# Four attention layers on one core: finishing each item's output later, spreading the Q/K projection, projecting V once, and zeroing on another engine

## The chip, the cores and the metric

One core of a Trainium2 chip. The metric is the device time of one execution in microseconds (us), on the slowest core, which here is the only one. Each profile also gives the clock that was granted to TensorE (PE), as a share of full speed, averaged over the run or over a stretch. In this case that clock takes only the values 0.5 ("cold") and 1.0 ("warm") at any moment (the traces of the two kernels have 244 stretches at each and none at another value), so a mean of 0.93 says that 14% of the time was cold. A stretch of time at 0.5 is called a cold spell below.

## The reference, cut to what matters

```python
def _A_ref(x, wqkv, wo):             # windowed layer; B is the same without the mask ("dense")
    qkv = (x @ wqkv).reshape(B, S, 3, H, Dh) ...      # S = 2048, D = 640, H = 32, Dh = 20
    scores = einsum("bhqd,bhkd->bhqk", q, k) * Dh**-0.5
    mask = (idx[:,None] - idx[None,:] >= 0) & (idx[:,None] - idx[None,:] < 256)
    p = softmax(where(mask, scores, -1e9))
    return einsum("bhqk,bhkd->bhqd", p, v) ... @ wo
x = x + A(layernorm(x)); x = x + B(layernorm(x))      # and both once more: four layers
```

## The kernel before

Everything stays in SBUF. A layer normalises x and transposes it to `xnT`. It then goes through eight groups `g` of four heads. In a group, each *item* is one block of 512 queries for two heads. It runs over its key blocks of 128 keys: 16 in a dense layer, 4 or 6 in a windowed one. For each key block it does S on PE (two heads of 32 rows each), exp on ScalarE (ACT), masks on VectorE (DVE), and PV on PE. V carries a column of ones, so PV also gives the softmax's sum. After the last key block comes the item's *tail*: copy out of PSUM, four transposes, and a division per head.

```python
        for g in range(G):                                       # 8 groups
            for tb in range(NT):                                 # V of this group: 80 columns wide
                vps = psA.tile([P, 4 * DH], F32, ...)
                for dc in range(KD): nc.tensor.matmul(vps[:], lhsT=xnT[...], rhs=stage[..., 80 cols])
                nc.vector.tensor_copy(out=v_g[:, tb, :, 0:DH], in_=vps[...])
            for which in range(2):                               # Q and K of this group
                for qsb in range(NQSB):
                    pps = psA.tile([P, QSB], F32, ...)
                    for dc in range(KD): nc.tensor.matmul(pps[:], lhsT=wpad[:, dc, g, :], ...)
                    nc.vector.tensor_copy(out=qkT[:, which, ...], in_=pps[:])
            for qsb in range(NQSB):
                for s in range(2):                               # one item
                    oT_ps = psB.tile([32, 2, QSB], F32, ...)
                    for ki, kc in enumerate(kcs):
                        # S: two matmuls, 32 rows each
                        for j in range(2):
                            nc.tensor.matmul(s_ps[:, j, c0:c1],
                                lhsT=qkT[slot : slot + 32, 1, ...], rhs=qkT[slot : slot + 32, 0, ...],
                                tile_position=(slot, 0), ...)
                        pt = ptp.tile([P, 2, QSB], BF16, ...)    # 3 buffers
                        if windowed and (c0 > 0 or c1 < QSB):
                            nc.gpsimd.memset(pt[:], 0.0)         # the whole tile
                        nc.scalar.activation(out=pt[:, :, c0:c1], in_=s_ps[:, :, c0:c1], func=ACT.Exp)
                        # ... masks on VectorE ...
                        for j in range(2):
                            nc.tensor.matmul(oT_ps[0 : DH + 1, j, :], lhsT=v_g[:, kc, 2*s+j, :], rhs=pt[:, j, :], ...)
                    # tail: two copies, then four transposes from psB, each with two divisions
                    for j in range(2): nc.vector.tensor_copy(out=oT_sb[...], in_=oT_ps[0 : DH + 1, j, :])
                    for qb in range(4):
                        tr_ps = psB.tile([P, 64], BF16, ...)
                        nc.tensor.transpose(out=tr_ps[:], in_=oT_sb[0:64, ...], identity=ident[0:64, 0:64])
                        # ... reciprocal and scaling for two heads ...
        # ... output projection, residual add
```

The softmax here doesn't subtract the row's maximum and nothing guards it: scores larger than these inputs give would overflow.

## Time and profile before

4597.9 us is the median of 15 runs (4588.2 to 4606.5). The runs agree well, and every one has a mean clock near 0.82. This is where the profiled run spends it; attention runs from a layer's first exp to its last, and a boundary is what lies between:

| stage | us | clock |
|---|---|---|
| start to first exp | 61.7 | |
| windowed attention, first / second | 711.0 / 707.2 | 0.72 / 0.72 |
| dense attention, first / second | 1391.1 / 1405.6 | 0.88 / 0.86 |
| three boundaries between layers | 88.7, 86.7, 87.4 | |
| end | 60.5 | |

From the page of the kernel before: the clock in 40 slices (in tenths), the shares of the chain that ended last, by engine, and four of the costliest groups (busy us, mean ns of one, then idle time ahead of them and what ended most of it).

```profile
PEclk8776777888988888988867677777888898888888
PE 44%; ACT 26%; DVE 15%; issue 12%; POOL 2%; DMA 1%; ACTq 0%; POOLq 0%; DVEq 0%
L235 ACT ACTIVATE pt<-s_ps 128x1024 bf16<-128x1024 f32 (+2 forms) x2752 | 2429.5, 915 | 1785.4 <-PE s_ps L224 715.6
L267 PE MATMUL oT_ps<-pt,v_g 128*21 128x512 bf16 x5504 | 1920.6, 461 | 351.9 <-ACT pt L235 182.3
L276 DVE CAST oT_sb<-oT_ps 21x512 bf16<-21x512 f32 x512 | 347.8, 679 | 2000.4 <-PE oT_ps L267 1996.9
L234 POOL MEMSET pt<- 128x1024 bf16 x704 | 645.8, 952 | 1080.6 <-PE oT_ps L267 1019.0
```

The exp, the largest single job, leaves ScalarE idle for 1785 us. The chain of the end goes through VectorE and "issue" for 27% of the time, which is what handing work to and fro costs. And the clock row contains sixes and sevens in the two windowed stretches: there PE was busy 73% of the time at a mean clock of 0.72, in the dense ones 85 and 86% at 0.88 and 0.86.

### The profile page before, as it was taken

Reading aid. Unit: us, or ns where it says so; the run is one execution under the profiler, and the core shown is the slowest. Engines: PE = TensorE matmul, PEld = TensorE weight load, DVE = VectorE, ACT = ScalarE, POOL = GpSimd, SP = SyncE. Lnnn points to the kernel's source line nnn. Section 1 sums busy time; section 2 is a strip of 40 time slices with the busy share of each in tenths; the row PEclk is TensorE's granted clock in tenths of the full one; section 3 lists DMA queues with packets and bytes.
Section 4 is the critical chain, followed back from the end, with each engine's and each line's share of the span. In section 5 each row is a group of like instructions: output and inputs, shape, how many; then the busy total and the mean of one; then the engine's idle time right before and its main releaser. Section 6 shows DMA issues by size and latency. Waiting matters only on the chain.

```text
span 4599.8 us, 48782 instructions
## 1 busy us (share of the span) xinstructions
PE 3690.3 (80%) x17152; PEld 1242.5 (27%) x17152; DVE 1673.3 (36%) x7465; ACT 2458.6 (53%) x2824; POOL 666.8 (14%) x748
## 2 busy tenths in 40 slices
PE   5777777788888888888777777768888888888886
PEld 2222222322222222222322222232222222222223
DVE  6555556421222212212465555563212212212223
ACT  2222322467677676676422232225676676676773
POOL 3434443000000000000034444420000000000000
PEclk8776777888988888988867677777888898888888
DMA  1000000000000000000000000000000000000000
GB/s 52 1 1 1 1 1 22 8 1 0 1 1 1 1 0 1 1 1 22 1 8 1 1 1 1 22 8 1 1 1 1 1 1 1 1 1 1 1 0 23
DMA packets 9622, 21.46 MB, mean 5 GB/s; under 512 B 160, under 2 KB 6816, under 8 KB 9376
## 3 DMA queue, kind: packets, MB, share of 16 engines
q1 hardware_dynamic: 9376, 18.35, 1.1%
q8 instruction: 134, 2.20, 0.2%
q14 instruction: 112, 0.92, 0.1%
HBM read 15.73 MB, written 2.62 MB: 4 GB/s over the span
## 4 chain that ended last, share of the span: by engine, by line
PE 44%; ACT 26%; DVE 15%; issue 12%; POOL 2%; DMA 1%; ACTq 0%; POOLq 0%; DVEq 0%
ACT pt L235 26%; PE oT_ps L267 24%; PE s_ps L224 9%; PE pps L193 6%; DVE oT_sb L276 5%; POOL pt L234 2%; PE vps L176 2%; DVE o_sb L293 2%; PE y_ps L310 2%; DVE rz L290 1%; DVE pt L259 1%; PE tr_ps L282 1%; DVE pt L246 1%; DVE v_g L183 1%; DVE x_sb L317 1%
## 5 line engine op out<-in xcount | busy, mean ns | idle before, releaser
L235 ACT ACTIVATE pt<-s_ps 128x1024 bf16<-128x1024 f32 (+2 forms) x2752 | 2429.5, 915 | 1785.4 <-PE s_ps L224 715.6
L267 PE MATMUL oT_ps<-pt,v_g 128*21 128x512 bf16 x5504 | 1920.6, 461 | 351.9 <-ACT pt L235 182.3
L224 PE MATMUL s_ps<-qkT 32*128 32x512 bf16 (+3 forms) x5504 | 1146.6, 386 | 213.1 <-ACT pt L235 183.6
L276 DVE CAST oT_sb<-oT_ps 21x512 bf16<-21x512 f32 x512 | 347.8, 679 | 2000.4 <-PE oT_ps L267 1996.9
L267 PEld LDWEIGHTS <-v_g 128*21 128x21 bf16 x5504 | 502.4, 101 | 1159.7 <-issue 913.1
L234 POOL MEMSET pt<- 128x1024 bf16 x704 | 645.8, 952 | 1080.6 <-PE oT_ps L267 1019.0
L224 PEld LDWEIGHTS <-qkT 32*128 32x128 bf16 x5504 | 283.7, 92 | 1298.0 <-issue 1273.1
L293 DVE TENSOR_SCALAR o_sb<-tr_ps,rz 128x20 bf16<-128x20 bf16 x2048 | 403.4, 222 | 24.4
L172 POOL MEMSET v_g<- 128x64 bf16 x32 | 12.2, 381 | 2437.7 <-PE oT_ps L267 2437.7
L282 PE MATMUL tr_ps<-ident,oT_sb 64*128 64x64 bf16 x1024 | 175.0, 212 | 209.1 <-DVE oT_sb L276 111.9
L290 DVE RECIPROCAL rz<-tr_ps 128x1 f32<-128x1 bf16 x2048 | 302.7, 159 | 100.1 <-PE tr_ps L282 75.3
L246 DVE TENSOR_TENSOR pt<-pt,mask_ge 128x256 bf16<-128x256 bf16 x512 | 146.8, 287 | 361.6 <-ACT pt L235 361.1
L200 DVE CAST qkT<-pps 128x512 bf16<-128x512 f32 x256 | 177.0, 691 | 121.9 <-PE pps L193 121.7
L282 PEld LDWEIGHTS <-oT_sb 64*128 64x128 bf16 x1024 | 79.4, 97 | 496.2 <-DVE oT_sb L276 184.5
L183 DVE CAST v_g<-vps 128x80 bf16<-128x80 f32 x512 | 118.2, 236 | 251.1 <-PE vps L176 233.2
L176 PE MATMUL vps<-stage,xnT 128*128 128x80 bf16 x2560 | 187.4, 218 | 22.0 <-DVE v_g L183 11.5
L176 PEld LDWEIGHTS <-xnT 128*128 128x128 bf16 x2560 | 139.5, 108 | 82.7 <-issue 56.8
L193 PE MATMUL pps<-xnT,wq_pad 128*128 128x512 bf16 x640 | 149.8, 391 | 0.0
L193 PE MATMUL pps<-xnT,wk_pad 128*128 128x512 bf16 x640 | 143.4, 379 | 0.0
L141 ACT ACTIVATE rstd<-mv,eps_t 128x1 f32<-128x1 f32 x64 | 18.8, 294 | 221.0 <-DVE mv L139 117.9
L259 DVE TENSOR_TENSOR pt<-pt,mask_lt 128x256 bf16<-128x256 bf16 x448 | 118.7, 283 | 3.0
L310 PE MATMUL y_ps<-wo_sb,oTd 128*128 128x320 bf16 x640 | 119.0, 316 | 0.0
(33 smaller groups left out, 700.0 us busy)
## 6 DMA issues: line engine op xcount, KB each, us to landing
stage<-in_A_wqkv_dram SPq DMA_DIRECT2D x2, 2400.0 KB, 12.0
stage<-in_B_wqkv_dram SPq DMA_DIRECT2D x2, 2400.0 KB, 9.0
x_sb<-in_A_x_dram SPq DMA_DIRECT2D x1, 2560.0 KB, 9.8
out_dram<-x_sb SPq DMA_DIRECT2D x1, 2560.0 KB, 8.7
wo_sb<-in_A_wo_dram SPq DMA_DIRECT2D x2, 800.0 KB, 9.8
wo_sb<-in_B_wo_dram SPq DMA_DIRECT2D x2, 800.0 KB, 4.5
```

The source lines that it names most:

```text
L176: nc.tensor.matmul(vps[:], lhsT=xnT[:, dc, tb * P : (tb + 1) * P], rhs=stage[:, dc, 2 * D + g * 4 * DH : 2 * D + (g + 1) * 4 * DH], start= ...
L193: nc.tensor.matmul(pps[:], lhsT=wpad[:, dc, g, :], rhs=xnT[:, dc, qsb * QSB : (qsb + 1) * QSB], start=(dc == 0), stop=(dc == KD - 1),)
L224: nc.tensor.matmul(s_ps[:, j, c0:c1], lhsT=qkT[slot : slot + 32, 1, kc * P : (kc + 1) * P], rhs=qkT[slot : slot + 32, 0, qsb * QSB + c0 : ...
L234: nc.gpsimd.memset(pt[:], 0.0)
L235: nc.scalar.activation(out=pt[:, :, c0:c1], in_=s_ps[:, :, c0:c1], func=ACT.Exp)
L246: nc.vector.tensor_tensor(out=pt[:, :, qb_diag * P : (qb_diag + 1) * P], in0=pt[:, :, qb_diag * P : (qb_diag + 1) * P], in1=mview, op=ALU. ...
L267: nc.tensor.matmul(oT_ps[0 : DH + 1, j, :], lhsT=v_g[:, kc, h_in_g, :], rhs=pt[:, j, :], start=(ki == 0), stop=(ki == len(kcs) - 1),)
L276: nc.vector.tensor_copy(out=oT_sb[32 * j : 32 * j + DH + 1, :], in_=oT_ps[0 : DH + 1, j, :],)
L282: nc.tensor.transpose(out=tr_ps[:], in_=oT_sb[0:64, qb * P : (qb + 1) * P], identity=ident[0:64, 0:64],)
L290: nc.vector.reciprocal(out=rz[:], in_=tr_ps[:, 32 * j + DH : 32 * j + DH + 1])
L293: nc.vector.tensor_scalar_mul(out=o_sb[:, qsb * 4 + qb, hh * DH : (hh + 1) * DH], in0=tr_ps[:, 32 * j : 32 * j + DH], scalar1=rz[:, 0:1],)
L310: nc.tensor.matmul(y_ps[:, i, 0 : D // 2], lhsT=oTd[:, dc, :], rhs=wo_sb[:, dc, i * (D // 2) : (i + 1) * (D // 2)], start=(dc == 0), stop= ...
```

## The change

Its intent: keep PE and ScalarE going across the ends of items and groups. The tail of an item is emitted after the next item's loop, with its own PSUM pool. A group's Q and K are projected in four portions during the group before. V is projected for all heads at once at the layer's start, into a store with zero columns, so that both heads add into one 64-row PSUM tile and one copy empties it. The zeroing of `pt` moves from GpSimd (POOL) to VectorE and covers only the columns that the exp leaves out. Cut to its core:

```diff
-    vp = ctx.enter_context(tc.tile_pool(name="vp", bufs=2))
+    psC = ctx.enter_context(tc.tile_pool(name="psC", bufs=2, space=bass.MemoryType.PSUM))
+    v_all = big.tile([P, NT, H // 2, 96], BF16, name="v_all", tag="v_all")
+    def emit_tail(item):
+        oT_ps, hA, qsb, s = item
+        nc.vector.tensor_copy(out=oT_sb[:], in_=oT_ps[:])        # one copy for both heads
+        for qb in range(4): ...                                  # transposes (from psC), divisions as before
...
+        if lidx == 0:
+            nc.gpsimd.memset(v_all[:], 0.0)
+            # ... and the columns of ones
+        for tb in range(NT):
+            for h2 in range(2):
+                vps = psC.tile([P, 16 * DH], F32, name="vps", tag="c")      # 320 columns
...
+        emit_qk_proj(0, list(range(NQSB)))
+        pending = None
         for g in range(G):
-            # V projection of the group, QK projection of the group
             for qsb in range(NQSB):
                 for s in range(2):
-                    oT_ps = psB.tile([32, 2, QSB], F32, name="oT_ps", tag="o")
+                    oT_ps = psB.tile([64, QSB], F32, name="oT_ps", tag="o")
...
-                        if windowed and (c0 > 0 or c1 < QSB):
-                            nc.gpsimd.memset(pt[:], 0.0)
+                        if windowed and c0 > 0:
+                            nc.vector.memset(pt[:, :, 0:c0], 0.0)
+                        if windowed and c1 < QSB:
+                            nc.vector.memset(pt[:, :, c1:QSB], 0.0)
...
-                                oT_ps[0 : DH + 1, j, :],
-                                lhsT=v_g[:, kc, h_in_g, :],
+                                oT_ps[:],
+                                lhsT=v_all[:, kc, hA // 2, 32 * j : 32 * j + 64],
...
-                    # tail at once
+                    if pending is not None:
+                        emit_tail(pending)
+                    pending = (oT_ps, hA, qsb, s)
+                if g + 1 < G:
+                    emit_qk_proj(g + 1, [qsb])
```

## The prediction

> **What bounds the kernel now.** I read the page's 40 slices, then busy time by stage, then ScalarE's order of time inside one dense and one windowed layer, then the chain of waits over the same stretches. The stages (attention of the windowed layer, boundary, attention of the dense layer, last projection), from the windows view:
>
> ```profile
> 60.00:775.00 715.00, 523.92 (x2501) 182.74 (x2500) 399.36 (x1795) 214.65 (x354) 322.78 (x357) 0.72 0.01 4
> 775.00:859.00 84.00, 62.79 (x442) 38.44 (x443) 70.25 (x312) 4.71 (x16) 0.00 (x0) 0.80 0.03 11
> 859.00:2265.00 1406.00, 1197.07 (x5235) 368.54 (x5233) 304.11 (x1351) 1004.98 (x1027) 5.81 (x11) 0.88 0.01 2
> 4548.00:4600.00 52.00, 27.01 (x223) 19.09 (x222) 26.35 (x91) 0.00 (x0) 0.00 (x0) 0.93 0.15 51
> ```
>
> After the stretch: length, busy us of PE, weight load, DVE, ACT, POOL, then the granted clock. The two layer pairs repeat, so the span is about 60 + 2 x 715 + 3 x 84 + 2 x 1407 + 45 = 4600. No engine fills either attention stage (ACT 1005 of 1406 is the most, if matmul busy is not trusted), so both are held by a chain.
>
> Dense layer, one item (one query block of two heads, 16 key blocks), ScalarE's timeline:
>
> ```profile
> 1141.76 1.94 ACT L235 ACTIVATE pt<-s_ps 128x1024 bf16<-128x1024 f32 x2 [3.00 <-PE oT_ps L267]
> 1144.86 14.47 ACT L235 ACTIVATE pt<-s_ps 128x1024 bf16<-128x1024 f32 x14 [1.17 <-PE s_ps L224]
> 1161.44 1.94 ACT L235 ACTIVATE pt<-s_ps 128x1024 bf16<-128x1024 f32 x2 [2.11 <-PE oT_ps L267]
> ```
>
> 16.41 us of exponentials, about 4 us of idle per item. What PE does in that idle, from the chain:
>
> ```profile
> 1138.80 0.58 PE s_ps L224
> 1139.38 0.16 PE tr_ps L282
> 1139.55 0.54 PE s_ps L224
> 1140.09 0.18 PE tr_ps L282
> 1140.29 0.17 DVE rz L290
> 1140.45 0.14 DVE o_sb L293
> 1140.59 0.04 issue
> 1140.63 3.58 PE oT_ps L267 x8
> ```
>
> The four transposes of the finished item stand in PE's queue ahead of the next item's PV matmuls, and wait for VectorE's evacuation and for each other's buffers. Then 8 PV matmuls run at 3.58/8 = 0.45 us each, against 0.26 in the steady loop: the clock has dropped. Items in this stretch repeat every 20.58 us (they start at 1099.46, 1120.05, 1140.63). Between groups ScalarE is idle another 18.29 us, during the V and QK projections.
>
> Windowed layer, start of one item, ScalarE waiting for GpSimd's zeroing:
>
> ```profile
> 311.94 0.12 PEld L267 LDWEIGHTS <-v_g 128*21 128x21 bf16 x2 [0.78 <-PE tr_ps L282]
> 311.97 2.72 PE L267 MATMUL oT_ps<-pt,v_g 128*21 128x512 bf16 x6 [0.68 <-DVE o_sb L293]
> 313.04 2.74 POOL L234 MEMSET pt<- 128x1024 bf16 x3 [4.46 <-PE oT_ps L267]
> 314.02 1.49 ACT L235 ACTIVATE pt<-s_ps 128x768 bf16<-128x768 f32 x2 [4.60 <-POOL pt L234]
> ```
>
> The same tail blocks PE; only after it do PV matmuls free the three pt buffers, then 0.95 us of memset, then exp. An item takes about 10.3 us and a group 91 us (715/8 is 89).
>
> [...] its granted clock is only 0.5 or 1.0, 0.72 on average in the windowed and 0.88 in the dense stage, and PV matmuls take 0.43 to 0.45 us or about 0.22 apart. [...] (101 ns at 21 columns, 92 at 128), so going from 21 to 64 columns should cost little. [...] No VectorE memset of such size is in this trace.
>
> **The change part by part.**
>
> 1. Deferred tail, in one PSUM bank of 64 rows. V is stored with zeros so that both heads accumulate into one tile: the number of PV matmuls and their 512 columns stay. One evacuation of 0.68 us replaces two (512 x 0.68 = 348 us of VectorE become 174). The transposes now come two to four key blocks into the next item, as the PE order shows, with their own PSUM pool. The 4 us of idle per dense item should go almost entirely. Dense floor: the exp repeats every 14.47/14 = 1.034 us; PE's loop of S, PV needs 0.32 + 0.08 + 0.52 = 0.92 when warm. So 16 x 1.04 = 16.6 us per item.
>
> 2. QK projection spread over the previous group. In the dense layers the order puts one projection matmul after every second key block, harmless at 0.22 us. But the last four stand between the final PV matmuls, with the next item's S behind them: 0.43 + 0.52 + 0.34 + handoffs, about 1.4 us of idle ScalarE every second item. Per group 8 x 16.6 + 4 x 1.4 = 138.4, against 176 (1407/8). Eight groups: about 1110 per dense layer, saving 297, or 594 for both.
>
> 3. V projection once per layer. 2560 matmuls of 80 columns become 640 of 320: 160 per layer at 320/512 x 0.216 = 0.134 us = 21.4 us, plus a cold start and handoffs, about 25 us. It stands wholly before attention (160 in a row), where formerly 4 to 5 us did. Each of four starts grows by about 20: start 80, each boundary 105. The 128x24576 GpSimd memset, scaled from 4.37 us for 5120 elements, takes 21 us once, during the first normalisation: hidden.
>
> 4. Zeroing moves from GpSimd (704 x 0.95 us) to VectorE, over the uncovered columns only. [...] VectorE per such item, start to start as the chain spaces them: evacuation 0.69, eight reciprocals x 0.075 = 0.6, eight scalings x 0.135 = 1.08, eight masks x 0.21 = 1.68, [...] one QK copy 0.69: 6.7 us. PE warm: six PV pairs x 0.52 = 3.1, S 1.3, transposes 0.6, projection 1.1: 6.1. ScalarE only 3.6. VectorE and PE are nearly equal and in order, each with waits for the other inside the item (third transpose behind scaling, memset behind PV), and some cold clock remains: I choose 8.3 us, 25% over the larger. The two items of a group's first query block have four key blocks: 6.9. Group 2 x (6.9 + 3 x 8.3) = 63.6, layer 510. Saves 205 each, 410 together.
>
> Sum: 80 + 510 + 105 + 1110 + 105 + 510 + 105 + 1110 + 59 (last tail, projection, store) = 3694. Against 4600: 594 + 410 saved, about 85 given back, the rest rounding. I predict 3690.
>
> **The rivals.** (a) VectorE becomes the hard bound of the windowed layers through the memsets: 6.7 us is already the largest sum, and in-order queues couple it to PE. If each item costs 9.5 us the layers lose 150 together: 3840. Against it: the tail wait that vanishes is worth about 5 us per item. (b) The windowed PE stays cold as now: its 6 us become up to 11, [...] at a mean clock of 0.8 it is near rival (a). (c) The deferred transposes only move the wait: each still waits for VectorE, now between S and PV. In the dense layers VectorE is 22% busy and PE waits for the exp at that place anyway; if 0.5 us per item leaked out, 2 x 64 x 0.5 = 64 us more. (d) Everything flows: windowed items at 7.0 us and no projection bubble, 2 x 80 + 2 x 45 less, about 3450. (e) The weight loads of 64 columns cannot hide[...], but only where PE binds.
>
> **Range and chances.** The windowed item (7.2 to 9.2 us, about +-60 per layer) and the dense item (+-35 per layer) dominate: 3690, range 3530 to 3850. Even with all of rivals (a), (c) and (e) the time stays under 4100, 11% faster. Faster 0.98, same 0.01, slower 0.01.
>
> **What would show it.** Right: exp repeating without a 3 us hole between dense items, dense attention about 1110 us with ScalarE over 88% busy and clock above 0.95; windowed attention near 510 us with VectorE the busiest engine at 75 to 85%, ScalarE no longer released by POOL; a 25 us block of V matmuls before each attention. Wrong: holes of ScalarE in the dense stage ended by transposes; windowed items above 9.3 us; a clock still at 0.72 there; [...] PV pairs longer than 0.52.

## The result, and the profile after

3802.0 us is the median of 11 runs (3736.6 to 3824.1). The ratio of the changed kernel to the one before is 0.818 (95% interval 0.8145 to 0.8211). Ratios here are the mean time of a kernel's fast runs over that of the kernel before in the same rounds, so not quite the ratio of the medians. This holds for the experiments too: the changed kernel did not run in their rounds, and is compared with them through its own 0.818, or by the mean of its fast runs, 3760 us.

Unlike before, the runs differ by 2%, and the time goes with the clock: 3746 us at a mean clock of 0.932, 3824 us at 0.907. On a single core there is no second die to compare with; the runs marked slow, seven of twelve, are those over 1.5% above the fastest, and each has a lower mean clock. So the median is the time of a slow run. The profile is of a fast one, with 3746 us (span 3744.5):

| stage | before | predicted | after | clock after |
|---|---|---|---|---|
| start to first exp | 61.7 | 80 | 100.5 | |
| windowed attention 1 | 711.0 | 510 | 440.8 | 0.97 |
| boundary | 88.7 | 105 | 112.8 | |
| dense attention 1 | 1391.1 | 1110 | 1179.4 | 0.94 |
| boundary | 86.7 | 105 | 110.4 | |
| windowed attention 2 | 707.2 | 510 | 468.4 | 0.88 |
| boundary | 87.4 | 105 | 115.3 | |
| dense attention 2 | 1405.6 | 1110 | 1157.9 | 0.96 |
| end | 60.5 | 59 | 59.0 | |
| sum | 4599.9 | 3694 | 3744.5 | |

The page of the changed kernel, the lines that answer to those of before:

```profile
PEclk9999998779799999999989999687999979999999
PE 58%; ACT 29%; DVE 10%; issue 3%; DMA 0%; ACTq 0%; DVEq 0%
L280 ACT ACTIVATE pt<-s_ps 128x1024 bf16<-128x1024 f32 (+2 forms) x2752 | 2469.6, 916 | 812.4 <-PE s_ps L267 411.9
L311 PE MATMUL oT_ps<-pt,v_all 128*64 128x512 bf16 x5504 | 1765.5, 401 | 240.9 <-ACT pt L280 103.2
L118 DVE CAST oT_sb<-oT_ps 64x512 bf16<-64x512 f32 x256 | 173.5, 678 | 1167.1 <-PE oT_ps L311 1167.0
```

ScalarE's idle time ahead of the exp fell from 1785 to 812 us, and VectorE and issue from 27% of the chain to 13%. The copy out of PSUM takes the same 0.68 us on 64 partitions as on 21, and there are half as many. GpSimd no longer zeroes `pt`. The clock row is mostly nines; the few eights, sevens and the six hold the cold spells.

Windows of the changed kernel (the stretch, its length, then busy us of PE, weight load, VectorE, ScalarE and GpSimd, the granted clock, DMA share and GB/s): windowed attention 1, the boundary, dense attention 1.

```profile
100.50:541.30 440.80, 394.98 (x1930) 145.01 (x1928) 366.33 (x1939) 209.69 (x352) 0.00 (x0) 0.97 0.00 1
541.30:654.10 112.80, 85.22 (x537) 47.87 (x536) 91.29 (x390) 7.34 (x20) 0.00 (x0) 0.86 0.08 30
654.10:1833.50 1179.40, 1094.58 (x4622) 324.64 (x4622) 234.92 (x1139) 1024.02 (x1024) 0.00 (x0) 0.94 0.00 1
```

In the windowed stage VectorE is busy 83% (366 of 441) and PE 90%; in the dense one ScalarE is busy 87% (1024 of 1179) and PE 93%, part of it at half speed. No engine is full, but two are close in each.

ScalarE's timeline in a warm part of the dense stage, one item without and one with a share of the projection (start, us, what ran, and in brackets the idle ahead of it and what ended it):

```profile
1027.35 1.94 ACT L280 ACTIVATE pt<-s_ps 128x1024 bf16<-128x1024 f32 x2 [1.78 <-PE s_ps L267]
1029.44 12.47 ACT L280 ACTIVATE pt<-s_ps 128x1024 bf16<-128x1024 f32 x12 [0.15 <-PE s_ps L267]
...
1062.86 1.94 ACT L280 ACTIVATE pt<-s_ps 128x1024 bf16<-128x1024 f32 x2 [1.77 <-PE s_ps L267]
```

The 3 and 2 us holes of before, ended by PV after the tail, are gone. What remains is one hole of 1.8 us in every second item, 35.5 us apart, ended by an S matmul: there the last four projection matmuls stand ahead of S. Item starts are 16.7 and 18.5 us apart when warm, so a warm group takes 141 us.

Now a stretch of the same stage that is not warm. PE's timeline of the changed kernel just after such a projection item:

```profile
779.29 0.19 PE L121 MATMUL tr_ps<-ident,oT_sb 64*128 64x64 bf16 x1 [0.17 <-DVE qkT L237]
779.96 0.59 PE L311 MATMUL oT_ps<-pt,v_all 128*64 128x512 bf16 x2 [0.48 <-ACT pt L280]
...
782.04 1.01 PE L311 MATMUL oT_ps<-pt,v_all 128*64 128x512 bf16 x2
782.99 0.61 PE L267 MATMUL s_ps<-qkT 32*128 32x512 bf16 x2
783.53 1.06 PE L311 MATMUL oT_ps<-pt,v_all 128*64 128x512 bf16 x2
```

Two short waits (0.17 and 0.48 us), and about 2 us later the PV pair takes 1.0 instead of 0.6 us: the clock is halved. In the 3.41 us up to then (window 778.62 to 782.03) PE was busy for 2.74 us, and its longest wait was the 0.48 us. The window over the spell shows that nothing is waited for any more:

```profile
782.00:833.10 51.10, 51.06 (x135) 9.68 (x134) 5.57 (x24) 29.64 (x29) 0.00 (x0) 0.50 0.00 0
```

For 51 us PE is 100% busy at half speed, and ScalarE only 58%. The pair of items in it takes 23.2 + 31.2 us where a warm pair takes 16.7 + 18.5, so one spell costs 19 us. The spell ends at the next pile of projection matmuls (four start between 829.6 and 832.0, and the clock is back at 833.2). There are three such spells in dense layer 1 and two in dense layer 2, and all five end at such a pile. This accounts for the dense stages: seven warm groups of 141.2 and a last one of 134 make 1122, plus 3 x 19 is 1179, and plus 2 x 19 is 1160.

### The profile page after: what moved, and what is told of

Its sections match the earlier page's. It is cut to its first block, busy times and chain, and to the rows that moved or that the text cites. A ratio compares the mean times of both kernels' runs of the same rounds, so it can differ in the third digit from the quotient of the medians.

```text
span 3744.5 us, 43991 instructions
## 1 busy us (share of the span) xinstructions
PE 3331.9 (89%) x15232; PEld 1135.2 (30%) x15232; DVE 1578.5 (42%) x7657; ACT 2498.7 (67%) x2824; POOL 33.3 (1%) x15
## 4 chain that ended last, share of the span: by engine, by line
PE 58%; ACT 29%; DVE 10%; issue 3%; DMA 0%; ACTq 0%; DVEq 0%
ACT pt L280 29%; PE oT_ps L311 28%; PE s_ps L267 12%; PE pps L230 9%; PE vps L207 3%; PE tr_ps L121 2%; PE y_ps L338 2%; DVE rz L129 2%; DVE pt L304 2%; DVE xn L180 1%; DVE x_sb L345 1%; DVE xnT L193 1%; DVE o_sb L132 1%; PE trp L331 1%; DVE pt L291 0%
## 5 line engine op out<-in xcount | busy, mean ns | idle before, releaser
L311 PE MATMUL oT_ps<-pt,v_all 128*64 128x512 bf16 x5504 | 1765.5, 401 | 240.9 <-ACT pt L280 103.2
L267 PE MATMUL s_ps<-qkT 32*128 32x512 bf16 (+3 forms) x5504 | 1049.7, 372 | 9.6 <-ACT pt L280 7.7
L311 PEld LDWEIGHTS <-v_all 128*64 128x64 bf16 x5504 | 506.2, 109 | 738.0 <-issue 577.9
L118 DVE CAST oT_sb<-oT_ps 64x512 bf16<-64x512 f32 x256 | 173.5, 678 | 1167.1 <-PE oT_ps L311 1167.0
L230 PE MATMUL pps<-xnT,wq_pad 128*128 128x512 bf16 x640 | 210.9, 408 | 0.0
L190 PE MATMUL trp<-ident,xn 128*128 128x128 bf16 x320 | 63.6, 260 | 77.9 <-DVE xnT L193 41.4
L331 PE MATMUL trp<-ident,o_sb 128*128 128x128 bf16 x320 | 63.6, 228 | 50.7 <-DVE oTd L334 47.9
L277 DVE MEMSET pt<- 128x128 uint32 (+2 forms) x384 | 104.3, 272 | 7.2 <-PE oT_ps L311 3.2
L207 PE MATMUL vps<-stage,xnT 128*128 128x320 bf16 x640 | 103.0, 315 | 0.5 <-DVE xnT L193 0.5
L230 PEld LDWEIGHTS <-wq_pad 128*128 128x128 bf16 x640 | 58.7, 99 | 118.9 <-issue 64.0
```

The costliest lines, as they stand in the source:

```text
L118: nc.vector.tensor_copy(out=oT_sb[:], in_=oT_ps[:])
L207: nc.tensor.matmul(vps[:], lhsT=xnT[:, dc, tb * P : (tb + 1) * P], rhs=stage[:, dc, 2 * D + h2 * 16 * DH : 2 * D + (h2 + 1) * 16 * DH], st ...
L230: nc.tensor.matmul(pps[:], lhsT=wpad[:, dc, gg, :], rhs=xnT[:, dc, qsb_ * QSB : (qsb_ + 1) * QSB], start=(dc == 0), stop=(dc == KD - 1),)
L267: nc.tensor.matmul(s_ps[:, j, c0:c1], lhsT=qkT[slot : slot + 32, 1, kc * P : (kc + 1) * P], rhs=qkT[slot : slot + 32, 0, qsb * QSB + c0 : ...
L311: nc.tensor.matmul(oT_ps[:], lhsT=v_all[:, kc, hA // 2, 32 * j : 32 * j + 64], rhs=pt[:, j, :], start=(ki == 0 and j == 0), stop=(ki == le ...
```

## The experiments

The theories. **A** (the prediction's): the gain is the holes that vanish, and the windowed layers are held by VectorE's memsets. **B**: the gain is held back by the PE clock. What decides is not how busy PE is but what it is busy with, so that large projection matmuls at regular intervals are worth more than the hole that they fill. All experiments start from the changed kernel, and each diff is against it.

### 1. The start: who zeroes V's store

```diff
+    nc.vector.memset(v_all[:], 0.0)         # at the top, before x has arrived; ones likewise
-            nc.gpsimd.memset(v_all[:], 0.0)
```

> The one GpSimd memset of v_all is replaced by VectorE memsets issued before x arrives; nothing else changes. Theory (the memset holds VectorE's normalising op for 19.82 us at the start): that op is back at 0.44 us, the first exp comes at about 80 to 86 us instead of 100.5, the time falls by 15 to 20 us, under one per cent. Rival (the stall lay in slack behind the weight load): first exp still near 100 us and no change of the time.

What it is about shows in the changed kernel's timelines of GpSimd and then VectorE at the start:

```profile
10.64 20.58 POOL L198 MEMSET v_all<- 128x24576 bf16 x1
```

```profile
14.35 19.82 DVE L180 TENSOR_SCALAR xn<-x_sb,rstd,nmr 128x640 bf16<-128x640 bf16 x2
```

Two normalising instructions, otherwise 0.44 us each, span 19.8 us together. The first ends just after this memset (31.2), the second just after GpSimd's two small memsets of the ones that follow it (34.0). By these times both were held until GpSimd's memsets ended; by what, no view shows.

Measured: 3744.1 us (3732.5 to 3776.9), ratio 0.815 [0.8104, 0.8205]. VectorE's timeline of the experiment:

```profile
3.46 10.30 DVE L67 MEMSET v_all<- 128x12288 uint32 x1 [2.53 <-issue]
16.71 0.33 DVE L153 TENSOR_SCALAR wq_pad<-stage 128x640 bf16<-128x640 bf16 x1 [2.95 <-DMA stage<-in_A_wqkv_dram]
25.31 0.80 DVE L183 TENSOR_SCALAR xn<-x_sb,rstd,nmr 128x640 bf16<-128x640 bf16 x2
```

The blocked pair is back to 0.80 us, so the blocking was the memset's. The same zeros took GpSimd 20.58 us as 24576 bf16 values and take VectorE 10.30 us as 12288 words, 0.84 ns for each value or word. But the first exp comes at 90.5 us, not at 80: the weight copies now stand in VectorE's queue ahead of the normalising and wait for their DMA. Half of the 20 us is had at the start. In the total they drown in the spread between runs.

### 2. The tail at once

```diff
-                    if pending is not None:
-                        emit_tail(pending)
-                    pending = (oT_ps, hA, qsb, s)
+                    emit_tail((oT_ps, hA, qsb, s))
```

> The tail (evacuation, four transposes, scalings) is emitted at once after each item, not one item later; one PSUM bank, own transpose pool, V once, spread QK projection and VectorE memsets stay. Theory A (the deferral carries most of the gain): dense items go from 16.7 and 18.5 us back to about 20, windowed ones from 6.0 and 8.1 to about 9, the total rises by 400 to 650 us to 4200 to 4450. Rival B (the separate PSUM pool for transposes already unblocks PE, since the scheduler orders by readiness): items within 1 us of the changed kernel, total under 3900.

Measured: 4171.5 us (4152.9 to 4229.3), ratio 0.906 [0.9034, 0.909]. ScalarE's timeline of the experiment at a warm boundary between items:

```profile
3005.92 1.94 ACT L280 ACTIVATE pt<-s_ps 128x1024 bf16<-128x1024 f32 x2 [3.24 <-PE s_ps L267]
```

The hole is back (3.2 us), but a warm group is only 148.5 us against 141: 7 us each, some 120 us over the 16 dense groups. The fast runs differ by 405 us (4165 against 3760 on average). The rest goes with the clock: 1228 us cold in 80 spells against 510 in 26 in the two profiled runs, with dense groups that hold a spell at 152 to 181 us, and windowed groups at 58 to 76 instead of 55. So the deferral is the largest of the parts that were taken back singly, and in the dense layers more through the clock than through the hole. In the windowed layers, where hardly a group stays warm, the two are not separated.

### 3. The projection at the front of the group

```diff
-        emit_qk_proj(0, list(range(NQSB)))
         for g in range(G):
+            emit_qk_proj(g, list(range(NQSB)))
...
-                if g + 1 < G:
-                    emit_qk_proj(g + 1, [qsb])
```

> The QK projection of a group stands again at the group's start; all else as changed. Theory A (as predicted, spreading is worth little more than it costs): every item at 16.7 us in the dense and 6.2 in the windowed layers, plus a gap of 9 to 11 us per group: dense group 133.7+10 = 144 against 141, windowed 49.5+10 = 59 against 55, total +60 to +120 us, about 3830 to 3880. Rival B (the scheduler pulls the front projection into the previous group by itself, because nothing holds it back): no gap of the exp at group starts and total within 1% of the changed kernel.

Measured: 4044.4 us (4015.7 to 4159.6), ratio 0.878 [0.8737, 0.8819], clock 0.805 to 0.853. A warm dense group takes 142.0 to 142.5 us, hardly more than 141, and a nearly warm windowed one 59 us instead of 55. By the holes alone the spreading is thus worth some 16 x 1 + 16 x 4 = 80 us of the 275 between the fast runs. But single dense groups take 210 us. Two windows of the experiment, inside a cold group and inside a warm one:

```profile
2650.00:2830.00 180.00, 180.00 (x490) 35.17 (x489) 21.37 (x119) 116.85 (x115) 0.00 (x0) 0.50 0.00 0
2860.00:2980.00 120.00, 108.34 (x492) 35.97 (x490) 21.37 (x119) 117.08 (x116) 0.00 (x0) 1.00 0.00 1
```

The same number of matmuls takes 180 us at 100% busy, or 120 us at 90% busy. Spells in the dense layers last 198 to 201 us: a whole group, until the next projection (20 matmuls of 128 rows in 4.5 us). In this dense loop a cold PE without a pause did not become warm by itself. (In the windowed layers of the same run it often does; experiment 7 comes back to this.)

### 4. The zeroing back on GpSimd

```diff
-                        if windowed and c0 > 0:
-                            nc.vector.memset(pt[:, :, 0:c0], 0.0)
-                        if windowed and c1 < QSB:
-                            nc.vector.memset(pt[:, :, c1:QSB], 0.0)
+                        if windowed and (c0 > 0 or c1 < QSB):
+                            nc.gpsimd.memset(pt[:], 0.0)
```

> Zeroing of pt goes back to GpSimd, whole tile, as before; all else as changed. Theory A (0.95 us of memset in the ring of three pt buffers binds): windowed items from 6.0 and 8.1 to 7.5 to 9 us, windowed layers 60 to 150 us longer each, total +120 to +300. Rival B (VectorE was the bound of the windowed layers, so taking 1.6 us per item from it helps): windowed layers no longer or shorter. The dense layers do not change in either.

Measured: 3739.2 us (3723.7 to 3802.8), ratio 0.812 [0.8101, 0.8146], windowed attention 442.9 and 439.7 us, a warm group 53.6 against 55.0. Moving the zeroing was worth nothing once the tail no longer held up the buffers. And since taking the memsets off VectorE, 2 x (0.165 + 0.272 + 0.378) = 1.6 us per six-block item by the rows of the changed kernel, shortens the item by no more than 0.2 us, VectorE probably does not bind the windowed layers either, for all its 83%. That is not shown by this run alone: a gain on VectorE and a loss to GpSimd's 0.95 us in the ring of three buffers could cancel (experiment 12 has six).

### 5. Which property of the matmuls: columns?

Experiment 3 (projection at the front) with PV's weights 128 columns wide instead of 64. The extra columns multiply other heads' V or zeros and land in unused PSUM rows, so the result stays right.

```diff
-                                lhsT=v_all[:, kc, hA // 2, 32 * j : 32 * j + 64],
+                                lhsT=v_pad[:, kc, 96 * (hA // 2) + 32 * j : 96 * (hA // 2) + 32 * j + P],
```

> The kernel with the QK projection at the group's start, whose cold spells last a whole group of 8 items (198 us), with the PV weights widened from 64 to 128 columns (rows 64 to 127 of the result are never read; the output stays right). Theory C (the clock comes back only when enough columns of the array work): cold groups of 210 us vanish or shrink, mean clock in the dense layers above 0.95. Rival R (columns don't count; it is the S matmuls on 32 rows, or the gaps at each switch between S and PV, that keep the clock down): dense groups are again either 142 or about 210 us, mean clock 0.80 to 0.90. Item times of warm groups should stay at 16.7 us in both, since the matmul's time goes with its 512 moving columns.

Measured: 4003.1 us (3913.5 to 4078.0), with three of four runs slow, so there is no ratio. The spells persist (198 us, cold groups of 207 us). The number of PV columns did not matter here, for the clock (spells of 198 us, as in experiment 3) or for the time of a warm group (141.6 to 142.2, against 142.0 to 142.5). Moving columns do: in the traces of the two kernels warm matmuls in a row start 35, 136 and 216 ns apart at 80, 320 and 512 of them, and two PV matmuls of 512 start 215 ns apart with 21 columns of weights as with 64.

### 6. Which property of the matmuls: rows?

Experiment 3 with S over all 128 rows instead of 32, which gives a wrong result (relative error 1.22).

```diff
-                                lhsT=qkT[slot : slot + 32, 1, kc * P : (kc + 1) * P],
-                                rhs=qkT[slot : slot + 32, 0, ...],
-                                tile_position=(slot, 0),
+                                lhsT=qkT[:, 1, kc * P : (kc + 1) * P],
+                                rhs=qkT[:, 0, ...],
```

> The same front-projection kernel, with S computed over all 128 rows (four heads summed; the result is WRONG on purpose) in place of 32-row tiles. Theory R (rows count): no dense item stays cold for longer than a few windows, no 198 us spell, mean clock above 0.95; warm items become PE-bound, since two full S matmuls cannot overlap: 16 x (0.43 + 0.52 + gaps) = 16.5 to 18 us. Rival C (columns of PV count) or rival G (gaps between S and PV count): cold groups persist, at about 25 to 30 us an item.

Measured: 3940.4 us (3937.8 to 3941.2), ratio 0.857 [0.8555, 0.858], clock 0.98. No dense spell lasts over 3.4 us. A warm item is longer (18.6 us against 16.7, as PE is now nearly full: in the changed kernel's trace two 32-row S matmuls start 3 ns apart, two warm PV matmuls on 128 rows 215 ns), yet by the two ratios the kernel is 2.4% faster than experiment 3, and its runs agree to 0.1%. Only one spell falls in each dense stage, right at its start, and it ends with S and PV alone; since PE is 95% busy when warm, it has fewer pauses that could start one (in the changed kernel's attention stages all 18 spells begin after 3.41 us in which PE was idle for 19% or more).

### 7. Rows, or the data in them?

The correct twin of experiment 6: K is copied into four tiles that are zero outside their own 32 rows, and S runs over all 128 rows of these.

```diff
+    kz = [big.tile([P, S], BF16, name=f"kz{i}", tag=f"kz{i}") for i in range(4)]     # zeroed once
+                            nc.vector.tensor_copy(out=kz[i][32 * i : 32 * i + 32, ...], in_=pps[32 * i : 32 * i + 32, :])
-                                lhsT=qkT[slot : slot + 32, 1, kc * P : (kc + 1) * P],
+                                lhsT=kz[2 * s + j][:, kc * P : (kc + 1) * P],
```

> The correct twin of the wrong-on-purpose run with S over all 128 rows: projection at the front of each group, S over 128 rows, but K copied into four tiles that are zero outside their own 32 rows, so that the result is right and only 32 of the 128 rows carry data. Theory T (what brings the clock back is that the instruction spans all 128 rows, whatever is in them): no cold spell over 15 us in the dense layers, dense clock above 0.99, dense item 18.6 us as in the wrong twin, warm group 158 to 166 (the four small K copies per block of queries lengthen the front), 3950 to 4020 us in all. Rival D (it is the data in the rows that count, as zero rows do no work): dense spells near 200 us as in the run with the projection at the front, dense clock 0.85 to 0.93, time above 4050. A third possibility, that the wrong twin kept its clock only since its saturated PE never idled, would show here as no cold spell at all after the first items of a dense layer, and can't be told from T by the time; a spell that starts and ends between projections speaks for T.

Measured: right result, 4081.4 us (4079.7 to 4081.6), ratio 0.889 [0.8871, 0.89], clock 0.972. The total misses theory T's range, since the front of the windowed groups was held up (68.5 us a group instead of 60). The 512 small copies are one possible reason; another, not tested, is that the four K tiles have one buffer each, where `qkT` has two. The clock is T's. The dense layers have no spell at all, which by the third reading on record tells little, since PE hardly idles there (it is 95% busy from 750 to 880). But each windowed layer has spells that begin after a hole at a group's start. Window over one of these, and over one of the two longest of experiment 3 in the same layer:

```profile
245.70:252.50 6.80, 5.55 (x16) 1.75 (x16) 3.60 (x19) 2.28 (x4) 0.00 (x0) 0.50 0.00 1
```

```profile
290.60:352.00 61.40, 59.85 (x187) 15.74 (x185) 36.79 (x206) 23.83 (x40) 0.00 (x0) 0.50 0.00 1
```

With full-row S the spell ends after 6.8 us, though PE was busy only 82% of it and no projection ran. With 32-row S it lasts 61 us at 97% busy. The pair alone would prove little, for of the 40 spells in experiment 3's windowed layers 32 last a single 3.4 us, and 29 end with no projection in their last window. But the traces say what differs. They are read in windows of 3.4 us, since all 242 cold spells that end within the traces of the two kernels last a whole multiple of 3.41 us (3.4 to 54.6 us in the changed kernel). Here are two stretches of 3.4 us of experiment 3, the first a windowed spell that ends with it, the second from inside a dense spell; all instructions, then those of S alone (length, busy us of PE and ScalarE, clock, DMA):

```profile
2256.63:2260.04 3.41, 3.41 (x12) 0.68 (x11) 2.51 (x9) 0.79 (x3) 0.00 (x0) 0.50 0.00 0
2650.00:2653.41 3.41, 3.41 (x11) 0.67 (x10) 0.00 (x0) 2.28 (x3) 0.00 (x0) 0.50 0.00 0
```

```profile
2256.63:2260.04 3.41, 0.77 (x6) 0.79 (x3) 0.50 0.00 0
2650.00:2653.41 3.41, 1.53 (x6) 2.28 (x3) 0.50 0.00 0
```

PE is 100% busy in both, and S takes 23% of the first and 45% of the second; the windowed layers have narrower S tiles beside PV of full width. Counted over all 330 cold windows of 3.4 us inside experiment 3's attention stages: where PE ran full-row matmuls, with neither 32-row S nor a transpose in progress, for at least 76% of the window, full clock followed in 33 of 33; below 72%, in 0 of 280; between, in 10 of 17. The share in which PE was busy at all does not tell them apart (median 1.00 in both). With full-row S that threshold is gone: all 19 cold windows of experiments 6 and 7 that contain S were followed by full clock, with PE at least 90% busy, though as little as 41% (experiment 6) and 45% (experiment 7) of the window lay outside S.

So in these runs the content of the rows did not count: with S on 128 rows, 96 of them zero, the spell shown ended after 6.8 us, and with S on 32 rows spells lasted 61 us and, in the dense layers, 198. Switching between tiled and full matmuls is not by itself what holds the clock down: with four or five such changes in a window, 19 windows of experiment 3 without projection were followed by full clock and 237 were not, and again the share divides them (0.73 to 0.80 against at most 0.74). These are counts over the traces, and no edit varied the share alone.

### 8. Projection in halves, one portion per item

```diff
-                if g + 1 < G:
-                    emit_qk_proj(g + 1, [qsb])
+                    if g + 1 < G:
+                        emit_qk_proj(g + 1, [qsb], (s,))     # Q after s = 0, K after s = 1
```

> The changed kernel, with the q projection of the next group after the first head pair of a query block and the k projection after the second, so that each item holds five projection matmuls and no pile of four at an item's end. If the 1.8 us that projection items cost (18.5 against 16.7) is the pile standing before the next S: warm dense items all at 16.7 to 17.0, dense group 134 to 136 against 141. Theory T (the clock needs a burst of full-array matmuls to return): cold spells then last longer than 51 us and the mean clock falls below 0.90, eating the gain, total 3750 to 3950. Rival (any projection matmul helps, and without the bubble at the item's end the clock never falls): clock above 0.95, total 3600 to 3680.

Measured: 3585.6 us (3571.0 to 3588.6), ratio 0.779 [0.7771, 0.781], below both ranges. The windowed layers did not gain (456 and 463 us). The window over dense attention 1 of the experiment:

```profile
672.30:1753.90 1081.60, 1014.74 (x4563) 315.25 (x4618) 234.55 (x1139) 1008.84 (x1025) 0.00 (x0) 1.00 0.00 1
```

The clock is 1.00 in the whole stage, ScalarE is 93% busy, items take 16.9 and 17.1 us, and a group 135.4. The same matmuls in smaller portions both halve the pile and give PE a portion of full-row work in every item. The two can't be separated here, but the clock alone (no dense spell, against three and two) is worth 57 + 38 us.

### 9. Six buffers for `pt` instead of three

```diff
-    ptp = ctx.enter_context(tc.tile_pool(name="ptp", bufs=3))
+    ptp = ctx.enter_context(tc.tile_pool(name="ptp", bufs=6))
```

> The changed kernel with six pt buffers in place of three. In its windowed layers ScalarE waits most often for a PV matmul to free a pt buffer (0.2 to 0.8 us each). Theory (that ring binds the windowed layers): windowed items from 6.0 and 8.1 to 5.0 and 7.0, windowed layers 50 to 90 us shorter each, total down 2 to 4%. Rival (PE and VectorE fill the items, the pt wait is only where the queue shows): less than 1% of change. Dense layers unchanged.

Measured: 3654.6 us (3637.8 to 3662.3), ratio 0.794 [0.7911, 0.7958], but not as expected. The windowed layers went from 441 and 468 to 431 us each, and a warm windowed group from 55.0 to 54.2. Most of the gain came with fewer cold spells (clock 0.958 to 0.966), so that the total, 3% below the changed kernel, falls in the theory's range for another reason.

### 10. V projected per group, as before

```diff
-        for tb in range(NT):
-            for h2 in range(2):
-                vps = psC.tile([P, 16 * DH], F32, name="vps", tag="c")
+        def emit_v(g):                        # called at the start of each group
+            for tb in range(NT):
+                vps = psC.tile([P, 4 * DH], F32, name="vps", tag="c")
```

> The changed kernel with the V projection back at the start of each group, 80 matmuls of 80 columns, while the rest stays. As the prediction counted it: the block before attention shrinks by about 20 us per layer (boundary from about 112 to 92), and each group gains 4 to 6 us of PE work, 8 x 5 = 40 us per layer, part of it beside ScalarE: net +20 to +25 us per layer, +80 to +100 in all. Rival (the scheduler puts these matmuls into idle PE time of the previous group): no loss per group, total 60 to 80 us shorter. A change of the cold spells is possible either way, since these are full-array matmuls; groups are compared at the same clock.

Measured: 3845.1 us (3815.6 to 3856.4), ratio 0.836 [0.8314, 0.8399]. First exp at 77.1 instead of 100.5, boundaries of 86 to 91 instead of 110 to 115, and a warm dense group of 145.4 instead of 141.1. The V projection once per layer costs what was predicted at the layer's start and earns it back within its groups.

### 11. and 12. The parts that helped, together

Experiments 8 and 9, and V's gaps alone zeroed on VectorE at the top. Number 12 also has the zeroing of `pt` on GpSimd, as in experiment 4.

```diff
+    nc.vector.memset(v_all[:, :, :, DH:64], 0.0)           # gaps only; ones likewise
+    nc.vector.memset(v_all[:, :, :, 64 + DH : 96], 0.0)
```

> Meant as the best version: projection halves after each head pair, six pt buffers, and only the zero gaps of v_all filled, on VectorE, before x arrives. If the three gains add: windowed layers from 460 to about 430, dense 1080, first exp at 80 to 84 instead of 101: 3500 to 3540. If the pt ring no longer binds once the projections are spread (PE and VectorE fill the 7.1 us items): 3550 to 3570.

> The same as the best version with the zeroing of pt on GpSimd, whole tiles, so VectorE loses about 1.6 us per windowed item. If VectorE binds the windowed items there: they fall below 6.6 us, windowed layers 20 to 40 us shorter each. If PE binds them: no change within 0.5%. If GpSimd's 0.95 us per tile binds even with six buffers (6 x 0.95 = 5.7 us per item): items no lower than 5.9.

Measured: 3520.9 us (3508.0 to 3532.9), ratio 0.766 [0.7634, 0.7687], and with GpSimd 3509.5 us (3503.0 to 3513.7), ratio 0.764 [0.7617, 0.7662]. Both beat the two kernels, the one before by 23%, the changed one by over 6% (fast runs). Between them the difference lies inside the intervals. The dense layers run at clock 1.00 in 1080 to 1082 us, the windowed ones in 434 (GpSimd) and 441 us.

## Why the prediction was right or wrong

The time (3802, predicted 3690) lies in the range, but part of that is luck. Measured minus predicted, in the profiled run: start +20, windowed stages -69 and -42, dense stages +69 and +48, boundaries +8, +5 and +10. The errors sum to +50 only because -111 and +117 nearly cancel. The median lies another 56 us higher, in runs with a lower clock that were not profiled.

**Step 1, the deferred tail: right.** A warm dense item without projection takes 16.7 us, predicted 16.6. Experiment 2 shows it as the largest part of those tested. Rival (c), that the wait would only move, is refuted by the 0.15 to 0.17 us gaps inside items.

**Step 2, the spread projection: its hole right, its reason wrong.** The hole was predicted at 1.4 us in every second item and is 1.8; the warm group was put at 138.4 and takes 141. But a projection at the front would give 142 when warm (experiment 3). Of the 275 us that the spreading earns by the fast runs, about 80 are holes, most of them in the windowed layers. The rest goes with the clock (1245 us cold in experiment 3's profiled run, 510 here). A dense spell lasts 48 to 51 us instead of 200, for all five end at a pile of projection matmuls, and such a pile comes four times per group instead of once.

**Step 3, V once: right in its price, wrong in one word.** Boundaries were put at 105 and take 110 to 115, and experiment 10 confirms price and return. The matmuls of 320 columns were put at 134 ns and start 136 ns apart when warm. The memset that was "hidden" behind the first normalisation was not: it stopped it for 19.8 us. Of the +20 at the start, moving it gave back 10 (experiment 1); without the V block the start still takes 77.1 us against 61.7 before (experiment 10). The memset's length, 21 us, was right.

**Step 4, the windowed item: its term was mis-sized.** 8.3 us was chosen as 25% over the larger engine's sum, VectorE's 6.7. The memsets' share of that sum was the author's estimate, for which the trace before had no VectorE memset of such size to measure. Warm items take 6.03 us without projection and 8.07 with it, on average 7.05, that is 5% over VectorE's estimated 6.7, or 11% over 6.4, its sum with the memsets as measured. VectorE was 83% busy, within the expected 75 to 85%, but it was not the busiest engine, which the prediction had named it: PE was, with 90%. Experiments 4 and 12 show that relieving VectorE gains nothing resolvable. The memsets take 165, 272 and 378 ns for 128, 256 and 384 words by the rows of the changed kernel, 1.6 us per six-block item. Rival (d), "everything flows", named the windowed item's 7.0 us; rival (a) fell.

**Rival (b) and the dense clock: the step that failed.** The prediction expected a dense clock above 0.95 and ScalarE above 88%, and gave the dense stages no term for cold spells. That the dense stages would stay warm was the author's assumption; the trace before had them at 0.88 and 0.86. Measured were 0.94 and 0.96, 87%, and three and two spells of 19 us. With its warm groups 1122 instead of 1110, this is the whole +69 and +48. Rival (b) itself, a windowed clock as low as before (0.72), did not come: it was 0.97 and 0.88. Experiment 3 shows a saturated PE cold for 198 us. Experiments 5 to 7 show that here the columns and the data did not matter, and that S in 32-row tiles did: over 180 us of a cold dense group S is running for 39% of the time, and in experiment 3 full clock returned only where full-row matmuls had at least 72% of a window. **Rival (e)**, a price for 64-column weights, is not seen: the warm group is the same with 128 (141.6 to 142.2 us against 142.0 to 142.5). A weight load took 101 ns at 21 columns (PV before), 109 at 64 (PV after) and 92 at 128 (S before).

What stays open: how much a 32-row matmul counts, and why the number of spells differs from run to run (3737 to 3824 us for the same program).

## What to carry to other kernels

Before valuing a filled hole, look at the clock in the windows: here the same matmuls took 1.5 times as long (180 us against 120) while PE was "100% busy". Where much of PE's work is in 32-row tiles, look at the share of full-row work, not at "busy": spread that work through the loop, in every item rather than in a block (here the dense clock was 1.00 so, and a block per group left spells of 198 us), and compare variants at the same clock. A long memset on GpSimd beside VectorE's normalising was not hidden here (20.6 us, and two instructions of VectorE took 19.8 us instead of 0.80); look at the durations of VectorE's instructions under it.
